# A fixed TensorE order from chunk 2 on, and two chunks' merges side by side, in a recurrence with a feed-forward block

## The chip, the core and the metric

The kernel runs on one core of a Trainium2 chip. The core has five engines with a queue each: TensorE (PE in the profile; its weight loads are PEld), VectorE (DVE), ScalarE (ACT), GpSimd (POOL) and SyncE (SP), which here only issues DMAs; ScalarE issues some too. An engine works through its queue in order, and an instruction that waits holds up all behind it. The metric is the device time of one execution in microseconds (us). Before the change it was 904.21 us, the median of 14 runs (901.24 to 910.47).

## What is computed

Batch 4, 8 heads, 768 tokens, head dimension 40, all float32. For each head a 40 x 40 state is carried over the tokens; the outputs of all heads, 320 numbers for each of 3072 tokens, go through a feed-forward block with 2048 hidden units:

```python
for t in range(S):
    y[:, :, t] = einsum('bhd,bhde->bhe', rt, state)
    Sa = einsum('bhde,bhe->bhd', state, at)
    state = state * wt[:, :, None, :] - einsum('bhd,bhe->bhde', Sa, bt)
    state = state + einsum('bhd,bhe->bhde', vt, kt)
...
x = y.transpose(0, 2, 1, 3).reshape(B * S, H * D)
h = x @ w_in
out = (h * sigmoid(h)) @ w_out
```

## The kernel before

**Chunks and units.** The 768 tokens are cut into 12 chunks of 64 (numbered 0 to 11, `n` in the code). Each chunk has two units (`m` 0 and 1), a unit being two of the four batches. Inside a chunk the recurrence is turned into matrix products and the inverse of a 64 x 64 triangular matrix for each head; only a state, the tile GV, goes from chunk to chunk.

**Prepare** (`prepare`, `pre`) readies a chunk's inputs for each unit: `scale` (two scans, L339, and a reciprocal, L340, on VectorE), `reciprocals` and `scaled` (key and query scalings on GpSimd, L352, L367 or L363), `rest` (the other keys on GpSimd, L344, two squares on ScalarE for a check, L347 and L348, and the load of w for a later unit), and `scores`, which calls `between` (TensorE products `pm`, masked by VectorE at L290) and, for the second unit, stores them to DRAM as md. `prepare(n)` returns ten steps, five for each unit, and the lists of indices in the code pick their order. Chunks 5, 7, 9 and 11 are staged: their scaled queries wait in a tile `stage`, and `stack` copies them.

**Rows** (`invert`, `inverse`). For two chunks at once the scores come back from DRAM as mi, and VectorE inverts by substitution: each `row` is a product (L423) and a reduce (L430), and each needs the one before. Chunks 0 to 3 invert blocks of 16 (15 rows), later ones blocks of 32 (31 rows). `back` copies the result into mi, half on ScalarE (L439) and half on VectorE (L440), and sends it to DRAM as xd.

**Merge** (`merge`) puts a chunk's inverse together from its blocks. `fetch` loads XT from xd; `turned` transposes blocks on VectorE (L467). For chunks below 4, `corners` (TensorE products, a VectorE scaling into the tile qq, L488) and `complete` (TensorE products, a VectorE add at L518, four ScalarE copies at L523, a GpSimd memset) join the 16-blocks to 32-blocks. `first` and `second` (products `pq` and `po`, a pair of ScalarE copies after each, L542 and L560) join the 32-blocks to 64.

**Chain** (`chain`), six steps for each unit of a chunk: `keys` (TensorE transposes `pt`), `right` (`pr`), `solve` (`pu` and `pw`, with the inverse XT), `read` (`pl`, masked at L726), `write` (`pgy`; VectorE updates the state GV at L765 and L769 and makes the output yx at L774; ScalarE's queue sends yx to DRAM as xs) and `turn` (the state transposed into GT, by VectorE in even chunks from 2 on, L691, by TensorE in odd ones). `keyed` (`pm`, L312) makes part of the input of a chunk's `right`, and runs before it.

**Feed-forward** (`moe`). A pair of chunks is 512 token columns. When both chunks are written, `fetch` loads xs back as xt (issued by ScalarE, L800 and L802). A *first step* is six products into two banks (L817, L822) and two Silus on ScalarE (L824, tile gts); a *second step* is eight products (L829) that sum over half of the hidden units, with a copy (L838, or L843 and an add on GpSimd and the stores of out). The steps of a pair are numbered from 0: first steps 0 to 3, second 4 to 7, first 8 to 11, second 12 to 15. The pair of chunks 0 and 1 is cut by chunk, so it has 24: first steps of half width 0-3, 6-9 and 12-19, second steps 4-5, 10-11 and 20-23. All wait in one list `queue`; `take(n)` emits the next n.

**Order.** A planner at compile time puts each engine's instructions in order: by their place in the program, but what it reckons to be ready goes first when the engine would be free. `in_order` ties an instruction behind the last one of its line: feed-forward products are one line from the start; with `mark["pair"]` set, `product` ties every other TensorE product to the same line, and TensorE's order is the program's order. `behind` ties one instruction behind another on the same engine. For even chunks, once `mark["pair"]` is set, the VectorE instructions of `scale` are tied so: unit 0 behind `mark["row"]`, the last reduce of the rows, and unit 1 behind `mark["across"]`, the last transpose of an even chunk's merge. Weights arrive as 64-bit words and are converted on VectorE and ScalarE in 41 steps, `convert`, during the first 210 us.

**Stages.** Chunks 0 and 1 run one after the other, with 4 steps of the first pair's queue. Then 8 more steps are woven with prepare of chunks 2 and 3, their rows and the merge of chunk 2. A loop handles chunks 2 and 3 with TensorE's order left to the planner: chunk 2's solve is followed by chunk 3's merge; prepare of chunks 4 and 5 and the rows for both are woven in; 10 of the 12 steps left are given out, 16 new ones are added, `mark["pair"]` is set and 8 are taken (L1032). The loop at L1033 then makes four passes, for chunks 4-5, 6-7, 8-9 and 10-11. Each pass takes one step at seven places along its two chains (L1042 to L1066), one more before the second chunk's write, fetches xt and adds its own pair's 16 steps, takes two, turns the state, and takes six more beside the rows of the next two chunks. Those lines end a pass (L1071 to L1073):

```python
fetch, more = moe(n, xs)
x += [partial(fetch, 0), partial(queue.extend, more), partial(take, 2)] + turn
weave(x + [partial(take, 1)] * 6, rows[1:36])
```

In the fourth pass there are no further rows; the new steps are added and `run(queue)` (L1081) empties the list: the tail.

Of the kernel before, what the change touches and what calls it, by code (L numbers as in the profile page):

```python
# [9 lines left out]
F32 = mybir.dt.float32  # L10
# [31 lines left out]
def kernel(  # L42
# [355 lines left out]
    def inverse(md, N, queue, lo=0, hi=128):  # L398
        steps = []
        xd = dr.tile([128, 32, 32], F32, name="xd", bufs=2)  # L400

        if lo == 0:
            mark["tiles"] = [sb.tile([128, 2 * SKIP], F32, name="mi"), sb.tile([128, 32 * 32], F32, name="tmp")]
        mif, tmp = mark["tiles"]
        mi = mif[:, 0 : 32 * 32].rearrange("p (s t) -> p s t", s=32)
        I = 32 // N
        tmp = tmp[:, 0 : I * N * N].rearrange("p (i s t) -> p i s t", i=I, s=N)

        def blocks(x):
            x = x.rearrange("p (i x) -> p i x", x=SKIP)[:, :, 0 : 16 * 32] if N == 16 else x[:, 0 : 32 * 32].unsqueeze(1)  # L410
            return x.rearrange("p i (s t) -> p i s t", t=32)

        X, M = blocks(XIf), blocks(mif)
        for h in range(lo, hi, 64):
            mark["mi"] = send(queue, mi[h : h + 64], md[h : h + 64]).ins
        L = slice(lo, hi)

        pin = partial(in_order, line="vector") if hi - lo == 64 else lambda x: x

        def row(t):  # L420
            n = N - 1 - t
# [8 lines left out]
            x = nc.vector.tensor_reduce(out=X[L, :, t + 1 : N, t], in_=part, axis=AX.X, op=ALU.add)  # L430
            pin(x)
            mark["row"] = x.ins

        for t in reversed(range(N - 1)):
            steps.append(partial(row, t))

        def back():
            turned = XI.rearrange("p t s -> p s t")
            nc.scalar.copy(out=mi[L, 0:16], in_=turned[L, 0:16])  # L439
            pin(nc.vector.tensor_copy(out=mi[L, 16:32], in_=turned[L, 16:32]))  # L440
            send(queue, xd[L], mi[L])

        steps.append(back)
        return steps, xd

    def merge(n, xd, queue):
# [17 lines left out]
        def turned():  # L464
            for r in range(0, 128, 32 if small(n) else 64):
                c = r % 64
                x = nc.vector.transpose(out=X[r : r + 32, :, 32 - c : 64 - c], in_=X[r : r + 32, :, c : c + 32])  # L467
                pin(x)
                if n % 2 == 0:
                    mark["across"] = x.ins  # L470
            box["qq"] = sb.tile([128, N, 48], F32, name="qq", tag="tmp" if n > 0 else "xt")


        def corners():
# [17 lines left out]
        def complete():  # L492
            pp = box["qq"][:, :, 32:48]
            pe = bank("po")
            for h in range(N):
                for r in range(0, 128, 32):
                    product(
                        nc.tensor.matmul,
                        pe[r : r + 16, h * 16 : h * 16 + 16],
                        lhsT=pp[r : r + 32, h, :],  # L500
                        rhs=X[r : r + 32, h, r % 64 + 16 : r % 64 + 32],
                        start=True,
                        stop=True,
                        tile_position=(r, r),
                    )
                for r in range(0, 128, 64):
                    product(
                        nc.tensor.matmul,
                        pe[r : r + 32, 256 + h * 16 : 272 + h * 16],
                        lhsT=X[r : r + 32, h, 0:32],  # L510
                        rhs=pp[r : r + 32, h, :],
                        start=True,
                        stop=True,
                        tile_position=(r, r),
                    )
            pe = pe.rearrange("p (z h t) -> p z h t", z=2, h=N)
            for r in range(0, 128, 64):
                pin(nc.vector.tensor_tensor(  # L518
                    out=X[r : r + 32, :, 32:48], in0=pe[r : r + 32, 1], in1=X[r : r + 32, :, 32:48], op=ALU.add
                ))  # L520
# [443 lines left out]
    for u in units[2] + units[3]:  # L964
# [7 lines left out]
    del queue[0:4]  # L972
    fetch(1)
    ahead = [prepare(n) for n in (2, 3)]
    weave(
        queue[0:8],
        [x[i] for x in ahead for i in (0, 5, 1, 6, 2, 7, 4, 9, 3, 8)] + [partial(keyed, u) for u in units[2]] + invert(3),
        convert[21:31],
    )
    del queue[0:8]  # L980
    for n in range(2, 4):
        for u in units[n]:
            load_v(u)
            load_r(u)
        for u in units[n + 2] if n == 3 else []:
            load(u)
        if n % 2 == 0:
            xs = dr.tile([DM, 4 * NM * C], F32, name="xs", bufs=2)
        steps = [x for pair in zip(*[chain(u, xs) for u in units[n]]) for x in pair]
# [16 lines left out]
        del queue[0:now]  # L1006
    for u in units[6]:
        load(u, "bk")
    fetch, more = moe(2, xs)
    fetch(0)  # L1010
    queue += more

    def each(what, n, *x):
        for u in units[n] if n < NN else []:
            what(u, *x)
# [220 lines left out]
```

## Time and profile before

| What | Value |
|---|---|
| median of 14 runs | 904.21 us (901.24 to 910.47) |
| profiled execution | 908.37 us, span 906.6 us, granted TensorE clock 0.908 |
| TensorE busy | 783.2 us, 86% of the span, 10914 instructions |
| VectorE busy | 555.7 us, 61% |
| ScalarE busy | 296.7 us, 33% |
| GpSimd busy | 150.8 us, 17% |
| chain of work that ended last | PE 52%, DVE 34%, DMA 5%, issue 3% |
| start of chunk 4's transposes | 373.3 us |
| passes of the loop, by the transposes that begin them | 124.8, 123.4 and 123.4 us, then 73.4 to the end of the last write |
| tail | from 818.2 us, 88 us |

The profile is one execution, recorded on the chip. The 40 slices are equal parts of the span; a digit is the busy share in tenths, and PEclk the granted TensorE clock in tenths. In an answer by time, a line gives the start in us, the time in us, engine, source line, operation, out<-in, shapes and count; in brackets stands how long the engine had been idle and what released it. A float32 product counts as two matmuls, so a second step is x16, a first step x8 (L817) and x4 (L822). "ACTq" is a DMA issued by ScalarE, "issue" time in which an engine waited for nothing that the profile shows. L268 is the helper `product`: go by the tile's name.

### The profile page before, as it was taken

What the parts mean: (1) busy time and instruction counts of PE and PEld (TensorE: products, weight loads), DVE (VectorE), ACT (ScalarE), POOL (GpSimd) and SP (SyncE); (2) the same over time, 40 slices, a digit from 0 to 9 for tenths busy, and PEclk for the clock granted to TensorE, in tenths of its full rate; (3) what the DMA queues carried; (4) which work ended last, traced back from release to release, by engine and by line L of the source; (5) the groups of instructions that cost most, each with busy time, mean ns of one, the idle gap of its engine ahead of it and who ended that gap; (6) DMA issues with size and microseconds to landing.
All of it is one profiled execution on the core that took longest, in us unless ns stands there. A gap on an engine that the chain in (4) does not pass through costs nothing.

```text
span 906.6 us, 25356 instructions
## 1 busy us (share of the span) xinstructions
PE 783.2 (86%) x10914; PEld 552.3 (61%) x10914; DVE 555.7 (61%) x1084; ACT 296.7 (33%) x689; POOL 150.8 (17%) x156
## 2 busy tenths in 40 slices
PE   2045689898889769999998999999999989999996
PEld 2034677675668563775854866747758557675544
DVE  9989989995107589529598276895395951610000
ACT  2234468552331311534122514115250234231120
POOL 7402024001020500224001304102140000000001
PEclk9655769999679688999999999999999999999999
DMA  8964636644033450362732454603624222202001
GB/s 171 202 144 133 155 90 158 159 124 116 19 75 84 102 138 24 68 149 67 162 86 47 109 115 93 158 8 81 142 51 112 65 47 40 55 9 72 1 1 31
DMA packets 240150, 82.99 MB, mean 92 GB/s; under 512 B 207136, under 2 KB 231968, under 8 KB 240032
## 3 DMA queue, kind: packets, MB, share of 16 engines
q1 hardware_dynamic: 219488, 69.96, 34.5%
q10 hardware_dynamic: 20544, 11.34, 4.7%
q8 instruction: 87, 1.43, 0.6%
q14 instruction: 31, 0.25, 0.1%
HBM read 67.11 MB, written 14.16 MB: 90 GB/s over the span
## 4 chain that ended last, share of the span: by engine, by line
PE 52%; DVE 34%; DMA 5%; issue 3%; SPq 3%; ACT 2%; POOL 1%; ACTq 0%; POOLq 0%; DVEq 0%
PE po L829 14%; PE ph L817 10%; DVE tmp L423 9%; DVE XI L430 8%; PE pgy L268 4%; DVE w L340 4%; PE pl L268 4%; PE ph L822 3%; PE po L268 3%; PE pm L268 3%; PE pr L268 3%; PE pq L268 3%; SPq L221 3%; PE pu L268 2%; PE pt L268 2%
## 5 line engine op out<-in xcount | busy, mean ns | idle before, releaser
L829 PE MATMUL po<-wo_s,gts 128*128 128x320 f32 x768 | 226.4, 450 | 10.0 <-ACT gts L824 8.1
L817 PE MATMUL ph<-xt,wi_s 128*128 128x512 f32 (+1 forms) x448 | 185.1, 555 | 15.1 <-DMA xt<-xs 8.8
L829 PEld LDWEIGHTS po<-wo_s,gts 128*128 128x128 f32 x768 | 146.2, 195 | 75.7 <-issue 10.9
L817 PEld LDWEIGHTS ph<-xt,wi_s 128*128 128x128 f32 x448 | 82.6, 195 | 97.4 <-issue 69.0
L824 ACT ACTIVATE gts<-ph 128x512 f32<-128x512 f32 (+1 forms) x112 | 54.5, 532 | 194.1 <-PE ph L822 192.5
L726 DVE TENSOR_TENSOR vl<-pl,ml 128x512 f32<-128x512 f32 x48 | 30.9, 685 | 111.7 <-PE pl L268 58.7
L423 DVE TENSOR_TENSOR tmp<-XI,mi 64x2 f32<-64x2 f32 (+40 forms) x169 | 84.5, 500 | 10.2 <-DMA mi<-md 5.6
L340 DVE RECIPROCAL w<-W 128x512 f32<-128x512 f32 x24 | 80.3, 3344 | 1.0
L430 DVE TENSOR_REDUCE XI<-tmp 64x2 f32<-64x2 f32 (+40 forms) x169 | 76.8, 454 | 4.8
L845 POOL TENSOR_TENSOR ot<-gts,ot 128x320 f32<-128x320 f32 x24 | 21.1, 877 | 326.5 <-ACT gts L843 326.5
L352 POOL TENSOR_TENSOR kb<-kb,w 128x512 f32<-128x512 f32 x20 | 25.4, 1269 | 217.7 <-DVE w L340 84.0
L822 PE MATMUL ph<-xt,wl_s 64*128 64x512 f32 (+1 forms) x224 | 57.9, 588 | 0.0
L268 PE MATMUL pm<-a,kb 64*64 64x64 f32 x1280 | 42.4, 247 | 16.4 <-POOL kb L370 15.5
L268 PEld LDWEIGHTS pm<-a,kb 64*64 64x64 f32 x1280 | 39.1, 160 | 22.0 <-POOL kb L370 15.7
L268 PE MATMUL pq<-XT,sb 32*32 32x32 f32 (+1 forms) x1280 | 29.9, 202 | 25.7 <-DVE XT L467 15.1
L843 ACT COPY gts<-po 128x320 f32<-128x320 f32 x24 | 10.2, 425 | 125.8 <-PE po L829 102.4
L268 PE MATMUL pl<-r,vut 64*128 64x64 f32 x768 | 46.5, 274 | 2.3 <-ACT vl L654 2.3
L367 POOL TENSOR_TENSOR a<-a,W 64x512 f32<-64x512 f32 x32 | 38.7, 1210 | 56.1 <-DMA a<-in_aT 34.1
L268 PEld LDWEIGHTS pl<-r,vut 64*128 64x128 f32 x768 | 44.7, 189 | 4.7 <-ACT vl L654 2.4
L268 PEld LDWEIGHTS pq<-XT,sb 32*32 32x32 f32 (+1 forms) x1280 | 27.1, 124 | 32.4 <-issue 15.9
L268 PE MATMUL pt<-ident,kb 128*128 128x128 f32 x192 | 26.7, 297 | 23.2 <-DVE a L312 23.2
L312 DVE TENSOR_TENSOR a<-pm,ml 64x512 f32<-64x512 f32 x48 | 33.0, 688 | 19.8 <-PE pm L268 19.1
(108 smaller groups left out, 1036.6 us busy)
## 6 DMA issues: line engine op xcount, KB each, us to landing
kb<-in_bT SPq DMA_DIRECT2D x48, 128.0 KB
vut<-in_vT SPq DMA_DIRECT2D x48, 128.0 KB
r<-in_rT SPq DMA_DIRECT2D x24, 256.0 KB
w<-in_wT SPq DMA_DIRECT2D x45, 128.0 KB
kb<-in_kT SPq DMA_DIRECT2D x44, 128.0 KB
a<-in_aT SPq DMA_DIRECT2D x32, 128.0 KB
vl<-in_v SPq DMA_DIRECT2D x48, 80.0 KB
xs<-yx ACTq DMA_DIRECT2D x48, 80.0 KB
```

Of the source, the lines that this page charges most:

```text
L221: x = queue.dma_start(out, in_)
L268: x = what(*x, **y)
L312: x = nc.vector.tensor_tensor(out=u.a[O, j], in0=pm[O].rearrange("p (q t) -> p q t", q=Q), in1=ml[O].unsqueeze(1).to_broadcast([C, Q, C]), ...
L340: pin(nc.vector.reciprocal(R, u.W[:, :, 1 : C + 1]))
L367: nc.gpsimd.tensor_tensor(out=u.a[J, j], in0=u.a[J, j], in1=u.W[J, :, 0:C], op=ALU.mult)
L423: x = nc.vector.tensor_tensor(out=part, in0=X[L, :, t + 1 : N, t + 1 : N], in1=M[L, :, t, t + 1 : N].unsqueeze(2).to_broadcast([hi - lo, I ...
L430: x = nc.vector.tensor_reduce(out=X[L, :, t + 1 : N, t], in_=part, axis=AX.X, op=ALU.add)
L726: nc.vector.tensor_tensor(out=u.vl[:, :, j, D:], in0=pl[j].rearrange("p (q t) -> p q t", q=Q), in1=ml.unsqueeze(1).to_broadcast([128, Q, C ...
L817: in_order(nc.tensor.matmul(ph[n], lhsT=wi_s[:, k, at : at + 128], rhs=xt[:, k, :], start=k == 0, stop=False))
L822: in_order(nc.tensor.matmul(ph[n], lhsT=wl_s[R, i, :], rhs=xt[R, 2, :], start=False, stop=True))
L824: nc.scalar.activation(out=place(2 * i + n)[:, T], in_=ph[n], func=AF.Silu)
L829: in_order(nc.tensor.matmul(po[:, 0:DM], lhsT=place(f)[:, b * 128 : b * 128 + 128], rhs=wo_s[:, NF // 2 * half + f, :], start=f == 0, stop ...
```

## The change

- In `back`, where the rows cover 128 partitions and blocks of 16 (chunks 2 and 3), ScalarE's half of the copy goes away and VectorE copies all of it. In every case `mark["row"]` is now VectorE's copy in `back`, and no longer the last reduce.
- The merge of chunk 3 gets its qq in another buffer (tag "mi"), and `mark["across"]` is also set by its add in `complete`.
- The weave of eight steps ends with the fetches of the inverses (`rows[0:19]`); chunk 2's merge leaves it.
- The loop over chunks 2 and 3 is replaced by a written-out order like that of the later loop, with `mark["pair"]` set from chunk 2's keys on: four steps, keys and right, then the merges of both chunks in turns, with chunk 2's solves between chunk 3's last products. `prepare(4)` comes after that and is tied behind the rows and the add as in the later passes. Feed-forward steps are taken at eight marked places, and eight more beside the rows of chunks 4 and 5. Loads of chunks 4, 5 and 6 move with it; the strict order on SP's queue (`issued["sync"]`) begins when the rows of chunks 4 and 5 fetch their scores.
- The passes from chunk 4 on are the same text as before.

```diff
         def back():
             turned = XI.rearrange("p t s -> p s t")
-            nc.scalar.copy(out=mi[L, 0:16], in_=turned[L, 0:16])
-            pin(nc.vector.tensor_copy(out=mi[L, 16:32], in_=turned[L, 16:32]))
+            at = 0
+            if N == 32 or hi - lo == 64:
+                at = 16
+                nc.scalar.copy(out=mi[L, 0:16], in_=turned[L, 0:16])
+            x = nc.vector.tensor_copy(out=mi[L, at:32], in_=turned[L, at:32])
+            pin(x)
+            mark["row"] = x.ins
             send(queue, xd[L], mi[L])
...
-            box["qq"] = sb.tile([128, N, 48], F32, name="qq", tag="tmp" if n > 0 else "xt")
+            box["qq"] = sb.tile([128, N, 48], F32, name="qq", tag={0: "xt", 3: "mi"}.get(n, "tmp"))
...
+                pin(x)
+                if n == 3:
+                    mark["across"] = x.ins
...
     ahead = [prepare(n) for n in (2, 3)]
+    rows = invert(3)
     weave(
         queue[0:8],
-        [x[i] for x in ahead for i in (0, 5, 1, 6, 2, 7, 4, 9, 3, 8)] + [partial(keyed, u) for u in units[2]] + invert(3),
+        [x[i] for x in ahead for i in (0, 5, 1, 6, 2, 7, 4, 9, 3, 8)] + [partial(keyed, u) for u in units[2]] + rows[0:19],
         convert[21:31],
     )
     del queue[0:8]
-    for n in range(2, 4):
...
-        now = {2: 6, 3: 4}[n]
-        x = prepare(n + 2)
-        if n == 2:
-            weave(steps[0:4], queue[0:1], convert[31:])
-            scores = [partial(load, u) for u in units[n + 2]] + [x[i] for i in (0, 5, 1, 6, 2, 4, 7, 9, 3, 8)]
-        else:
-            weave(steps[0:4], queue[0:1], [x[i] for i in (0, 5, 2, 7, 1, 6, 4, 9, 3, 8)])
-            scores = [partial(stack, u) for u in units[n + 2]]
-        rows = invert(n + 2)
-        merges = rows[35:]
-        weave(
-            steps[4:6] + late.pop(n, []) + [partial(keyed, u) for u in units[n + 1]] + steps[6:],
-            queue[1:now],
-            scores + rows[0:36],
-        )
-        del queue[0:now]
...
     mark["pair"] = True
+    xs = dr.tile([DM, 4 * NM * C], F32, name="xs", bufs=2)
+    keys, right, solve, read, write, turn = start(2)
+    each(load_v, 2)
+    each(load_r, 2)
+    weave(queue[0:4] + keys + right, convert[31:])
+    del queue[0:4]
+    each(load_v, 3)
+    each(load, 4)
+    each(load, 5)
+
+    one_, two = rows[19:24], late.pop(2)
+    take(1)
+    run(one_[0:2])
+    take(1)
+    run(two[0:1] + one_[2:3] + two[1:2] + one_[3:4] + two[2:3] + one_[4:5])
+    x = prepare(4)
+    run(two[3:4] + solve[0:1] + [x[i] for i in (0, 5, 1, 6)] + two[4:5] + solve[1:2] + [x[i] for i in (2, 7, 3, 8)])
+    each(keyed, 3)
+    run(read)
+    each(load_vut, 3)
+    take(1)
+    run(write + [x[i] for i in (4, 9)])
+    each(load_vl, 3)
+    x = prepare(5)
+    run([x[i] for i in (0, 2, 5, 7)] + turn)
+    keys, right, solve, read, write, turn = start(3)
+    run(keys + [x[i] for i in (1, 6)] + right)
+    take(1)
+    run(solve[0:1])
+    take(1)
+    run(solve[1:2] + [x[i] for i in (4, 9)])
+    rows = invert(5)
+    merges = rows[35:]
+    run(rows[0:1] + [x[i] for i in (3, 8)])
     issued["sync"] = mark["mi"]
     each(load_v, 4)
-    each(load_r, 4)
-    take(8)
+    each(load, 6, "bk")
+    run(read)
+    each(stack, 5)
+    x = [partial(each, load_vut, 4), partial(take, 1)]
+    x += write + [partial(each, load_vl, 4)] + [partial(keyed, u) for u in units[4]]
+    fetch, more = moe(2, xs)
+    x += [partial(fetch, 0), partial(queue.extend, more), partial(take, 2)] + turn
+    weave(x + [partial(take, 1)] * 8, rows[1:36])
```

More of the change, by code (lines that the diff above doesn't have):

```diff
@@ L517, in complete @@
             for r in range(0, 128, 64):
-                pin(nc.vector.tensor_tensor(
+                x = nc.vector.tensor_tensor(
                     out=X[r : r + 32, :, 32:48], in0=pe[r : r + 32, 1], in1=X[r : r + 32, :, 32:48], op=ALU.add
-                ))
+                )
+                pin(x)
+                if n == 3:
+                    mark["across"] = x.ins
                 nc.gpsimd.memset(X[r + 32 : r + 64, :, 0:32], 0.0)
@@ L980 @@
     del queue[0:8]
-    for n in range(2, 4):
[L982 to L989, printed above, removed]
-        now = {2: 6, 3: 4}[n]
-        x = prepare(n + 2)
-        if n == 2:
-            weave(steps[0:4], queue[0:1], convert[31:])
-            scores = [partial(load, u) for u in units[n + 2]] + [x[i] for i in (0, 5, 1, 6, 2, 4, 7, 9, 3, 8)]
-        else:
-            weave(steps[0:4], queue[0:1], [x[i] for i in (0, 5, 2, 7, 1, 6, 4, 9, 3, 8)])
-            scores = [partial(stack, u) for u in units[n + 2]]
-        rows = invert(n + 2)
-        merges = rows[35:]
-        weave(
-            steps[4:6] + late.pop(n, []) + [partial(keyed, u) for u in units[n + 1]] + steps[6:],
-            queue[1:now],
-            scores + rows[0:36],
-        )
-        del queue[0:now]
[L1007 to L1011, printed above, removed]
     def each(what, n, *x):
```

## The prediction

> **What bounds the kernel now.** I read the 40 slices first, then busy time by stage, then TensorE, ScalarE and VectorE in order of time.
>
> ```profile
> PE   2045689898889769999998999999999989999996
> DVE  9989989995107589529598276895395951610000
> PEclk9655769999679688999999999999999999999999
> ```
>
> VectorE is full to about 205 us, TensorE from about 365 us on; between them neither is, and TensorE's clock falls. By stage (columns: PE, PEld, DVE, ACT, POOL busy, clock, DMA share, GB/s):
>
> ```profile
> 214.00:373.30 159.30, 135.67 (x2269) 100.04 (x2269) 87.37 (x162) 40.44 (x94) 22.37 (x24) 0.81 0.34 77
> 373.30:498.10 124.80, 120.53 (x1602) 81.55 (x1601) 85.09 (x153) 39.69 (x89) 22.68 (x22) 0.99 0.43 97
> ```
>
> The first row is chunks 2 and 3: clock 0.81. The second is one pass of the loop for chunks 4 and 5: TensorE idles 4.3 of 124.8 us. The end of a pass, on TensorE and then on ScalarE:
>
> ```profile
> 452.79 8.88 PE L829 MATMUL po<-wo_s,gts 128*128 128x320 f32 x32
> 461.60 1.98 PE L268 MATMUL pt<-ident,GV 64*40 64x64 f32 x64
> 464.20 3.67 PE L817 MATMUL ph<-xt,wi_s 128*128 128x512 f32 x8 [0.62 <-DMA xt<-xs]
> ...
> 482.93 4.04 PE L829 MATMUL po<-wo_s,gts 128*128 128x320 f32 x14
> 490.19 6.80 PE L829 MATMUL po<-wo_s,gts 128*128 128x320 f32 x18 [3.22 <-ACT gts L824]
> 496.93 1.20 PE L268 MATMUL pq<-XT,sb 32*32 32x32 f32 x64
> ```
>
> ```profile
> 451.44 6.52 ACTq L780 DMA_DIRECT2D xs<-yx  x4
> ...
> 459.73 0.39 ACTq L800 DMA_DIRECT2D xt<-xs  x1
> ...
> 488.57 1.07 ACT L439 COPY mi<-XI 128x512 f32<-128x512 f32 x1 [4.94 <-DVE XI L430]
> 489.55 0.59 ACT L824 ACTIVATE gts<-ph 128x512 f32<-128x512 f32 x1
> ```
>
> The recurrence's output goes to DRAM (451-458), comes back as xt (issued 459.73), and the next pair's first feed-forward step starts at 464.20. Two second steps of the pair before (452.79, 8.88 us) and the turn (1.98) stand in that gap. The line at 488.57 shows the other bound: the rows' copy stands ahead of a Silu in ScalarE's queue.
>
> **The change part by part.** I add the new order from rows of before and set it against the same stretch.
>
> *The queue of steps.* After chunk 1, 12 steps remain in both. Before takes 18 of 28 (12 plus 16) by the loop's start: 10 left, as the trace shows (two second steps at 378.30 and 385.57 come first). The change takes 4, six singles, 2 and 8 = 20: 8 left. A pass takes 8, then adds 16 and takes two at once. Before, these two are old second steps; after, they are the new pair's first two first steps, which need xt. The order on TensorE is fixed, so turn, six more steps and the next merge queue behind this wait, and ScalarE's Silus and copies behind them.
>
> Chunks 2 and 3. Step 15 of the first queue ends at 211.05; the loop's first transposes are at 373.3: 162.3 us. After, up to chunk 3's transposes: keys and right 3.9 (1.90 + 2.00), three half-width first steps 7.95 (2.65 each), two corners 2.8 (1.41), two completes 5.2, four merge products 4.6 (1.15), solve 2.9, keyed 2.0, read 3.7, write 5.4, between 1.1: 39.6. Stalls: each complete shows about 2 us of issue (0.85 + 2.06 in one, 1.50 in the other): 4. Side by side, chunk 3's products cover most hops of chunk 2's merge; two stay bare, the wait of each chunk's first product for VectorE's add (0.9) and ScalarE's four copies (1.5), of which chunk 3's corners or chunk 2's second product cover about 0.9: 2 x 1.5 = 3. No wide step stands between step 17 and the read, so I take cold prices there: 0.6 to 1.0 per merge product (1.85, 2.19 at 238 and 243), 2.2 for the solve (5.1 at 312), 0.9 keyed (1.47 per 32 against 1.0): 7. Sum 53.7: chunk 3's transposes at 264.8, chunk 2's write ended at 263.7.
>
> Then VectorE and GpSimd lead: in the loop 19.2 us go by from the write's end (407.8) through scan, reciprocal and key scaling to the last reciprocal keys (427.0). So chunk 5's scores end at 283.8, three us after TensorE could. Read 3.7, second step 4.4, write 5.4, keyed 2.0: 299.4. From here as in a pass: xt after 11, four first steps 18.8 (4.69), four second 17.6 (4.40), one merge product 1.1: 347.9.
>
> The rows of chunks 4 and 5 start 9.9 after the scores (12.1 at 557.6, less the 2.2 that key loads then hold SP's queue ahead of the score stores; the change puts those loads behind the score fetch): 293.7. They take 43.8 as at 444.8 to 488.6, and 9.6 more to the transposes: 347.0. But:
>
> ```profile
> 339.07 0.59 DVE L440 COPY mi<-XI 128x512 f32<-128x512 f32 x1
> 339.57 0.42 DVE L430 TENSOR_REDUCE XI<-tmp 128x16 f32<-128x256 f32 x1
> ...
> 363.16 1.16 DVE L430 TENSOR_REDUCE XI<-tmp 128x31 f32<-128x961 f32 x1
> 364.23 1.28 DVE L339 TENSOR_TENSOR_SCAN W<-w,one 128x260 f32<-128x260 f32 x2
> ```
>
> VectorE's half of the copy runs after 15 of 31 rows, slipped between a product and its reduce. The next scan is pinned behind mark["row"], now this copy and no longer the last reduce, so 1.28 + 3.35 = 4.6 us can slip into the rows. I take it (the copy did the same): 351.6, a gain of 21.7 us. Bounds: nothing slips in, 25.4; cold and issue doubled, 15; all of VectorE's relief below arrives, 31.
>
> *Prepare(4) moves.* Two scans and reciprocals at 167.8, 169.6, 178.6, 179.8 (9.2 us), four squares on ScalarE, GpSimd's four key scalings at 202-211 and their w loads go behind the rows of chunk 3. There VectorE idles 5.3 us before the fetched inverses and more later, so they cost nothing; without that cover, 9.2. Rows 3 can then end up to 9.2 earlier (213.3), but TensorE is at 97% (150-214) with steps that need no rows, and keys, right and step 16 (6.6 after 211.05) end at 217.7, where corners could start at 222. I have used 217.7, so 4.4 is already in the sum.
>
> *Copy on one engine.* ScalarE's 1.07 beside VectorE's 0.60 becomes one VectorE copy of about 1.2: 0.1. It frees a Silu that held TensorE 2.49 at 214.67. *Second qq buffer, loads of chunks 4 and 5:* no work added; TensorE's 42 us from 222 to 264 covers their issues on SP (kb 5.2, a 3.5, GV 5 to 6). If a GV load waits on right and holds SP ahead of the inverse fetch, up to 5 us.
>
> *Three passes.* First step at 464.2, now after 11.4 us idle. Row: after 6.45 idle at 340.59 eight such products took 5.70 instead of 3.70, so 2.0 more. Then two first 9.4, turn 2.0, two first 9.4, four second 17.6: merge at 504.6, was 496.93: +7.65. The 4.6 in the rows is hidden (their inverses would serve 501.5). The 40.4 from xt to the merge added to the other passes' xt: 588.39 + 40.4 against 620.31 is +8.5, and 711.1 (issue 706.65 + the first pass's 4.47 to landing) + 40.4 against 743.71 is +7.8. Together +23.9. Bounds: 17 (never cold), 37 (the rows' copy ahead of Silus costs 4.3 in each).
>
> The Trainium skill, "TensorE: Matmul & The Clock Gate", Part 1 says that an idle window of about 3.4 us halves the clock and about 3.4 us of work restores it; this speaks against the change. By it four starts would lose at most 4 x 1.7 = 6.8 us, against 4 x 2.0 here. The trace parts from it on the gap: 2.49 us idle at 214.67 was enough (four products 1.85, were 1.13).
>
> *Tail.* Before, two second steps (8.88 at 818.20) end as xt lands; after, TensorE waits: two steps less, the same wait, 2.0 cold, 0.1 for the earlier issue: +1.9 (0 to 3).
>
> Sum: -21.7 + 23.9 + 1.9 = +4.1. The profiled execution took 908.37 us (span 906.6 and 1.8 around it), 4.2 above the median of 904.21 and inside the runs' spread (901.24 to 910.47); the difference is carried to the median: 908.3. I take 908.
>
> **Rivals.** *VectorE's relief carries through:* 9.2 us leave a full stretch, and ScalarE's Silus stop waiting on squares (2.13 and 1.27 of TensorE waits). Against: TensorE was 97% busy there. It decides once 6.8 of the 9.2 arrive (4.1 + 2.7); all of it gives 908.3 - 9.2 = 899. *The rows' copy blocks:* 488.57 stands ahead of a Silu already, and the steps come later by 11; against: with the scan the rows end later too. A second step that begins at 487 needs the last Silu by 490.6; behind a copy that starts at 493.2 it gets it at 494.9, so 4.3, and three times that: 921. *The steps don't stall:* xt is there when the two steps come up; for it only that transfers look short; against, 459.73 waits on stores that wait on the write. Then the entry's gain (21.7) and the two steps less in the tail (8.8) stay, while the scans, no longer hidden, cost 4.6 in each of two passes (9.2): 904.2 - 21.7 - 8.8 + 9.2 = 883.
>
> **How the numbers follow.** Main case 0.52, own range 901 to 915; relief 0.20; blocked copy 0.22; no stall 0.06. Two runs are told apart at 0.3% (2.7 us). Faster: 0.05 + 0.17 + 0.06 = 0.28; same: 0.15 + 0.03 = 0.18; slower: 0.32 + 0.22 = 0.54. The range 893 to 924 leaves out no stall and the far ends of two bounds (entry 15, passes 37).
>
> **What would show it.** Right: the loop's first chunk-4 transposes at 345-356; L817 idle 9 to 11 us on xt after keyed in each pass, its first products near 5.7; passes of 131 to 134 us; L339 between L423 and L430. Wrong: passes of 125, or the entry above 362 or below 342.

## The result and the profile after

The changed kernel takes 922.03 us (median of 10 runs, 916.35 to 928.44); the kernel before took 905.25 us in the same comparisons (47 runs). The ratio is 1.0188, with a 95% interval of 1.0160 to 1.0215: slower, by close to 2%. The profiled execution took 922.61 us, 920.7 of it span (before: 908.37 and 906.6). So the span grew by 14.1 us where the prediction's sum had 4.1. (The medians lie 16.8 us apart: the profile of before fell on an execution 3.1 us above the median of the 47, that of after on one 0.6 above its own.)

In the changed kernel the lines of the old code stand eight or so further down: L817 is now L825, L829 is L837, L780 is L788, L765 is L773. By stage (columns: PE, PEld, DVE, ACT, POOL busy, clock, DMA share, GB/s):

```profile
206.80:267.30 60.50, 47.97 (x1463) 42.56 (x1461) 31.25 (x50) 20.00 (x50) 11.42 (x12) 0.74 0.39 86
267.30:352.90 85.60, 82.06 (x848) 55.66 (x845) 68.99 (x123) 23.47 (x53) 16.09 (x16) 0.96 0.39 87
352.90:487.70 134.80, 121.36 (x1604) 81.90 (x1601) 86.94 (x154) 39.76 (x90) 23.63 (x23) 0.95 0.40 89
487.70:624.50 136.80, 122.10 (x1606) 82.45 (x1601) 84.36 (x152) 40.09 (x92) 23.30 (x23) 0.94 0.39 88
624.50:756.90 132.40, 121.79 (x1605) 81.87 (x1601) 76.12 (x148) 38.03 (x84) 19.52 (x20) 0.95 0.34 77
```

The first two rows are chunks 2 and 3; they end 20.4 us earlier than before (352.9 against 373.3). The other three are the passes for chunks 4 to 9: 134.8, 136.8 and 132.4 us where before they took 124.8, 123.4 and 123.4. TensorE's busy time in a pass is hardly changed (121.4 against 120.5 in the first); its idle time went from 4.3 to 13.4 us. What it waits for is the first line of the view of TensorE's waits (total, times, longest):

```profile
PE ph L825 <- DMA xt<-xs: 43.4, 5, 11.5
```

Here is the first pass on TensorE, from the key products of the next pair to the next pair's merge:

```profile
430.90 1.15 PE L268 MATMUL pm<-a,kb 64*64 64x64 f32 x32
433.43 1.15 PE L268 MATMUL pm<-a,kb 64*64 64x64 f32 x32 [1.37 <-DVE yx L782]
446.06 6.11 PE L825 MATMUL ph<-xt,wi_s 128*128 128x512 f32 x8 [11.48 <-DMA xt<-xs]
...
453.16 3.70 PE L825 MATMUL ph<-xt,wi_s 128*128 128x512 f32 x8
...
469.14 17.49 PE L837 MATMUL po<-wo_s,gts 128*128 128x320 f32 x64
486.57 1.20 PE L268 MATMUL pq<-XT,sb 32*32 32x32 f32 x64
```

Nothing stands between the key products and xt any more: 11.48 us of idle time. The first eight products after it take 6.11 us; eight of the same products take 3.70 one step later. The four second steps run without a gap (64 products in 17.49 us). ScalarE in that place:

```profile
469.25 1.09 ACT L832 ACTIVATE gts<-ph 128x512 f32<-128x512 f32 x2 [3.54 <-PE ph L830]
474.65 1.09 ACT L442 COPY mi<-XI 128x512 f32<-128x512 f32 x1 [4.32 <-DVE XI L430]
```

The rows' copy (474.65) comes behind the last Silus, not ahead of them. And VectorE ahead of the loop, where the half copy is the line at 312.79:

```profile
312.79 0.59 DVE L443 COPY mi<-XI 128x512 f32<-128x512 f32 x1
313.29 0.42 DVE L430 TENSOR_REDUCE XI<-tmp 128x16 f32<-128x256 f32 x1
313.62 0.69 DVE L339 TENSOR_TENSOR_SCAN W<-w,one 128x260 f32<-128x260 f32 x1
314.22 0.44 DVE L423 TENSOR_TENSOR tmp<-XI,mi 128x289 f32<-128x289 f32 x1
314.58 0.69 DVE L339 TENSOR_TENSOR_SCAN W<-w,one 128x260 f32<-128x260 f32 x1
315.19 0.43 DVE L430 TENSOR_REDUCE XI<-tmp 128x17 f32<-128x289 f32 x1
315.53 3.35 DVE L340 RECIPROCAL w<-W 128x512 f32<-128x512 f32 x1
```

Two scans and a reciprocal, 4.7 us of work, lie among the rows as soon as the half copy is done; passes 1 and 2 show the same, pass 3 does not.

### The profile page after: what moved, and what is told of

Its sections match the earlier page's. It is cut to its first block, busy times and chain, and to the rows that moved or that the text cites. A ratio compares the mean times of both kernels' runs of the same rounds, so it can differ in the third digit from the quotient of the medians.

```text
span 920.7 us, 25351 instructions
## 1 busy us (share of the span) xinstructions
PE 772.7 (84%) x10914; PEld 545.9 (59%) x10914; DVE 555.6 (60%) x1084; ACT 295.7 (32%) x688; POOL 150.7 (16%) x156
## 4 chain that ended last, share of the span: by engine, by line
PE 56%; DVE 26%; DMA 10%; issue 3%; ACT 2%; SPq 1%; ACTq 1%; POOLq 0%; DVEq 0%; POOL 0%
PE po L837 15%; PE ph L825 15%; DVE tmp L423 5%; DVE XI L430 5%; PE ph L830 4%; DVE w L340 4%; PE pl L268 4%; PE pgy L268 3%; DMA xs<-yx 3%; PE pu L268 3%; PE po L268 3%; PE pm L268 2%; PE pq L268 2%; PE pr L268 2%; PE pt L268 2%
## 5 line engine op out<-in xcount | busy, mean ns | idle before, releaser
L825 PE MATMUL ph<-xt,wi_s 128*128 128x512 f32 (+1 forms) x448 | 194.2, 580 | 45.4 <-DMA xt<-xs 43.4
L837 PE MATMUL po<-wo_s,gts 128*128 128x320 f32 x768 | 214.2, 436 | 0.0
L837 PEld LDWEIGHTS po<-wo_s,gts 128*128 128x128 f32 x768 | 143.6, 190 | 62.7 <-issue 4.9
L825 PEld LDWEIGHTS ph<-xt,wi_s 128*128 128x128 f32 x448 | 87.1, 204 | 128.9 <-issue 74.7
L347 ACT ACTIVATE junk<-w 128x512 bf16<-128x512 f32 x24 | 15.1, 631 | 110.6 <-DVE w L340 90.6
L851 ACT COPY gts<-po 128x320 f32<-128x320 f32 x24 | 10.2, 424 | 96.1 <-PE po L837 80.3
```

What stands on the lines that cost most here:

```text
L825: in_order(nc.tensor.matmul(ph[n], lhsT=wi_s[:, k, at : at + 128], rhs=xt[:, k, :], start=k == 0, stop=False))
L837: in_order(nc.tensor.matmul(po[:, 0:DM], lhsT=place(f)[:, b * 128 : b * 128 + 128], rhs=wo_s[:, NF // 2 * half + f, :], start=f == 0, stop ...
```

## The experiments

The theory after the result: the loop is entered with eight steps in the queue instead of ten, so each pass comes to xt with nothing to do, and that alone costs more than the entry gains. The rival: the new order on TensorE, with the merges side by side, is worse in itself. The table has the stages of every kernel's profile; they are cut where the key transposes (pt<-ident,kb) of chunks 3, 4, 6, 8 and 10 start, and the rest runs to the end of the span. The ratio is to the kernel before.

| kernel | chunk 3 at | entry (chunk 4 at) | pass 1 | pass 2 | pass 3 | rest | span | ratio (95%) |
|---|---|---|---|---|---|---|---|---|
| before | 288.4 | 373.3 | 124.8 | 123.4 | 123.4 | 161.8 | 906.6 | 1 |
| changed | 267.3 | 352.9 | 134.8 | 136.8 | 132.4 | 163.8 | 920.7 | 1.0188 (1.0160-1.0215) |
| e1: six takes | 266.9 | 352.0 | 130.2 | 130.0 | 124.3 | 161.7 | 898.3 | 0.9962 (0.9924-0.9999) |
| e2: six takes, old pin | 263.7 | 344.3 | 125.6 | 122.8 | 122.9 | 161.9 | 877.5 | 0.9757 (0.9697-0.9817) |
| e3: old pin alone | 267.1 | 349.8 | 140.7 | 136.9 | 130.8 | 165.3 | 923.5 | 1.0141 (1.0074-1.0208) |
| e4: before, ten takes | 279.0 | 371.0 | 134.6 | 135.8 | 130.8 | 163.8 | 936.0 | 1.0445 (1.0376-1.0514) |
| e5: products in the gap | 266.7 | 350.7 | 131.1 | 135.4 | 130.4 | 163.1 | 910.7 | 1.0156 (1.0066-1.0246) |
| e6: stores from GpSimd | 268.5 | 354.8 | 131.3 | 135.9 | 132.6 | 164.8 | 919.4 | 1.0172 (1.0100-1.0244) |
| e7: early scans | 274.6 | 360.7 | 135.2 | 134.0 | 132.7 | 163.5 | 926.1 | 1.0231 (1.0158-1.0303) |
| e9: merges in series | 266.8 | 356.0 | 136.8 | 136.0 | 132.7 | 164.0 | 925.5 | 1.0197 (1.0116-1.0279) |
| e10: e2 with GpSimd's stores | 269.0 | 354.5 | 126.3 | 123.9 | 123.7 | 162.2 | 890.6 | 0.9771 (0.9746-0.9796) |
| e11: seven takes, old pin | 268.9 | 348.2 | 127.7 | 131.5 | 126.9 | 163.7 | 898.0 | 0.9971 (0.9951-0.9992) |

How far a single profile may be trusted: the changed kernel, e1, e2, e3, e5 and e11 have the same program up to chunk 3's transposes, and start them between 263.7 and 268.9. An entry is therefore read to 3 us or so. The changed kernel, e7 and e9 have the same passes: the three together took 404.0, 401.9 and 405.5 us, a single pass up to 2.8 us more in one profile than in another.

### e1: six takes beside the rows

```
-    weave(x + [partial(take, 1)] * 8, rows[1:36])
+    weave(x + [partial(take, 1)] * 6, rows[1:36])
```

> The changed kernel with six instead of eight steps of the queue taken beside the rows of chunks 4 and 5, so that the loop is entered with ten steps left instead of eight and the last two steps of each pair again lie between the key products and the first product that needs xt. Theory (the passes are long because too few steps are left to cover xt): chunk 4's transposes at 348 to 352 us (the changed kernel 352.9), TensorE waits for xt 1 us or less in each pass (the changed kernel 6.1, 5.9, 6.6), passes of about 129, 128 and 124 us (134.8, 136.8, 132.4), tail after the last write 88 to 89 us (90.3), span about 895 us, ratio to the kernel before 0.98 to 0.995. Rival (the new order and the merges side by side cost the time themselves, wherever the steps lie): the passes stay at 132 us or more and the ratio at 1.01 or above.

The ratio is 0.9962, just above the 0.98 to 0.995 expected; passes 1 and 2 are 1 and 2 us longer than written down. Of the waits for xt, 43.4 us in the changed kernel, 2.2 are left, ahead of the loop; the passes are 4.6, 6.8 and 8.1 us shorter, the rest 2.1, and the entry is where it was. So two steps less ahead of the loop take 22 us off the span, and the rival, that the new order is bad in itself, is out. What TensorE meets in the first pass is the other bound:

```profile
433.37 8.88 PE L837 MATMUL po<-wo_s,gts 128*128 128x320 f32 x32
442.18 1.98 PE L268 MATMUL pt<-ident,GV 64*40 64x64 f32 x64
444.10 3.70 PE L825 MATMUL ph<-xt,wi_s 128*128 128x512 f32 x8
...
463.38 8.88 PE L837 MATMUL po<-wo_s,gts 128*128 128x320 f32 x32
479.16 0.31 PE L268 MATMUL pq<-XT,sb 32*32 32x32 f32 x2 [6.90 <-DVE XT L472]
```

Two second steps and the turn now fill the gap, and TensorE waits 6.90 us for the inverses that come from VectorE's rows instead.

### e4: the kernel before with ten takes

```
-    take(8)
+    take(10)
```

> The kernel before with ten instead of eight steps taken ahead of the loop, and nothing else of the change: the loop is entered with eight steps left. Theory (the number of steps left is what makes the passes longer, and the rest of the change earns 20 us at the entry): entry later by two steps of 4.4 us, about 382 us; TensorE waits for xt 5 to 7 us and a cold stretch of 2 us in each pass, passes longer by 7 to 10 us each, tail longer by 1.9; span 933 to 945 us, ratio 1.03 to 1.043. Rival (the number of steps left does no harm, since the same steps are only done earlier): ratio 0.997 to 1.003.

The ratio is 1.0445, just above the 1.03 to 1.043 expected, and the span 936.0. The kernel before, with nothing else changed, shows the passes of the changed one: 134.6, 135.8 and 130.8 us, and a rest longer by 2.0. The gap too:

```profile
451.55 1.85 PE L268 MATMUL pm<-a,kb 64*64 64x64 f32 x32 [1.77 <-DVE yx L774]
464.07 6.03 PE L817 MATMUL ph<-xt,wi_s 128*128 128x512 f32 x8 [10.67 <-DMA xt<-xs]
```

The sum of passes and rest is 31.6 us over before. The entry missed what was expected: 371.0, where 382 was written down. Chunk 3's transposes already started 9.4 us earlier than in the profile of before, at a higher granted clock (see the last section); from there to the entry it took 92.0 us against 84.9, 7.1 more, near the two steps of 4.4.

### e2 and e3: the pin of the scans

```
             pin(x)
-            mark["row"] = x.ins
+            if at == 0:
+                mark["row"] = x.ins
```

e2 has this and the six takes, e3 this alone.

> The kernel with six takes, and the row's mark set only in the two inverses whose copy is VectorE's alone, so that in the passes the scans (L339, L340) are held back behind the last reduction again and do not lie between the rows' instructions. Theory: with xt covered, the rows' chain is what sets the passes, so the 3 to 5 us of scans in passes 1 and 2 come off: passes of about 124.8, 123.4 and 123.4 us as before the change, entry at 347 to 352, span 880 to 888 us, ratio 0.97 to 0.98, and 4 us or more below the kernel with six takes alone. Rival (the scans lie in VectorE's idle time even then): within 2 us of the kernel with six takes alone.

> The changed kernel with the row's mark set only in the two inverses whose copy is VectorE's alone, the eight takes left. Theory (TensorE's waits for xt and the key products set the passes, and the scans are hidden beside TensorE's steps): within 2 us of the changed kernel, ratio 1.015 to 1.02. Rival (the scans between the rows, 3 to 5 us in each of passes 1 and 2, are the unpredicted part of the passes): 6 to 9 us less, ratio 1.008 to 1.012.

e2 has a ratio of 0.9757: faster than both kernels. The span, 877.5, is below the 880 to 888 expected, by an entry at 344.3 instead of 347 to 352. Its passes are those of the kernel before:

```profile
344.30:469.90 125.60, 122.39 (x1602) 83.39 (x1601) 83.97 (x151) 40.12 (x89) 22.86 (x22) 0.97 0.43 96
469.90:592.70 122.80, 118.90 (x1601) 80.58 (x1601) 84.54 (x152) 39.70 (x89) 22.70 (x22) 1.00 0.43 98
592.70:715.60 122.90, 118.99 (x1606) 80.68 (x1601) 80.18 (x150) 38.34 (x85) 20.38 (x20) 1.00 0.36 83
```

Against e1 they are shorter by 4.6, 7.2 and 1.4 us; the scans and the reciprocal among the rows were some 4.7 us in each of passes 1 and 2. The entry is 7.7 us earlier than in e1: 3.2 of it stand ahead of chunk 3's transposes already, and the other 4.5 are again the size of the scans, which are out of the rows ahead of the loop too. In e3 the same scans are out of the rows too (the first in pass 1 runs at 470.90, behind the last reduction at 469.83), yet its three passes together take 408.4 us against 404.0 in the changed kernel: nothing is gained. Its entry is 3.1 us earlier, but xt then comes 98.4 us after the start of pass 1 (93.2 in the changed kernel), which takes that back; why it comes so late there is not settled. The ratio of 1.0141 lies between what the two theories gave for e3, and its interval holds the changed kernel's 1.0188; the passes decide it. With eight steps left, TensorE and xt set the pass and the rows have time to spare; with ten, the rows set it and every us among them counts. One flaw hid the other.

### e11: seven takes, with the old pin

```
-    weave(x + [partial(take, 1)] * 6, rows[1:36])
+    weave(x + [partial(take, 1)] * 7, rows[1:36])
```

The diff is against e2.

> The kernel with the old pin of the scans and seven takes, so that nine steps are left at the loop's entry: half of the cover that the changed kernel gave up. Theory (cover is lost step by step): TensorE idles about 4 us ahead of xt in each pass, over the 2.95 us from which the first eight products were long in the runs so far, so these take 5.2 to 6.7 us; from xt to the next merge 37 us (33.3 with ten left, 40.3 with eight in the changed kernel); each pass about 4 us longer, the tail about 1; span 888 to 892 us, ratio 0.984 to 0.992. Rival (the rows of VectorE set the passes with more than 4 us to spare, so one step does no harm): within 3 us of the kernel with ten left, ratio 0.972 to 0.980.

The ratio is 0.9971: between e2 (0.9757) and e3 (1.0141), which have ten and eight steps left and the same pin; 0.984 to 0.992 was expected. Each step of cover that is missing costs about 2% here. The first product in pass 1:

```profile
439.46 5.07 PE L826 MATMUL ph<-xt,wi_s 128*128 128x512 f32 x8 [6.63 <-DMA xt<-xs]
```

I had expected 4 us of idle time; it was 6.6, 6.5 and 5.1 us. The two steps taken right before the turn are now one old second step and one new first step, and the turn (2.0 us) stands behind that first step, so it covers nothing. From xt to the next merge went 35.3, 36.6 and 36.0 us, about 1 less than expected (of the two numbers in the expectation's brackets, 33.3 is to the transposes behind the merge, 40.3 to the merge). The three passes are 14.8 us longer than e2's (12 expected), and the entry is 3.9 later than in e2's profile.

### e5: products in the gap

```
+    def warm(n):
+        t = moe_bank("ph")
+        for _ in range(n):
+            in_order(nc.tensor.matmul(t, lhsT=ident, rhs=wi_s[:, 0, 0:512], start=True, stop=True))
...
-            x += [partial(fetch, 0), partial(queue.extend, more), partial(take, 2)] + turn
+            x += [partial(fetch, 0), partial(queue.extend, more), partial(warm, 10), partial(take, 2)] + turn
...
+            warm(8)
```

> The changed kernel with products whose result nobody uses (ten in each pass, eight ahead of the tail; 128x512, about 0.43 us each) put on TensorE between the key products of the next pair and the first product that needs xt. They are work that the reference does not ask for; they fill part of the idle time, so that TensorE comes to xt with its clock up. Theory (the first eight products after the idle time cost 2.1 to 2.9 us more only because the clock has fallen): first eight products near 3.7 us instead of 6.11, 5.88, 6.61, 5.84; span 9 us below the changed kernel's 920.7, ratio to the kernel before 1.005 to 1.012. Rival (the length of these eight comes from xt landing in pieces, or from the loads of weights, and not from the clock): they stay near 6, ratio 1.017 to 1.021.

```profile
442.62 3.67 PE L825 MATMUL ph<-xt,wi_s 128*128 128x512 f32 x8 [2.05 <-DMA xt<-xs]
575.18 6.51 PE L825 MATMUL ph<-xt,wi_s 128*128 128x512 f32 x8 [3.31 <-DMA xt<-xs]
831.31 3.67 PE L825 MATMUL ph<-xt,wi_s 128*128 128x512 f32 x8 [2.90 <-DMA xt<-xs]
```

In passes 1 and 3 and in the tail the first eight products take 3.67 us, as in the middle of a run. In pass 2 the added products ended 3.31 us ahead of xt, and the eight took 6.51. The granted clock during these eight is 1.00 in pass 1 and 0.56 in pass 2 of e5, and 0.60, 0.62 and 0.55 in the three passes of the changed kernel. It is the clock, then, and neither how xt lands nor the weights. The three that came back are worth 2.44, 2.94 and 2.17, 7.6 us; passes and rest together are 7.8 us shorter than the changed kernel's (and 5.4 and 9.5 shorter than those of e7 and e9, which have the changed kernel's passes). One by one they do not match: the passes are 3.7, 1.4 and 2.0 us shorter and the rest 0.8, so the close sum is partly chance. The span's 10.0 includes an entry 2.2 earlier, which this edit does not touch. The ratio, 1.0156, is above the range expected, with an interval that holds that range's upper part and the changed kernel's ratio as well: the profile shows the price, the times alone do not.

### e6: the output's stores from GpSimd's queue

```
-                nc.sync.dma_start(out[at : at + C, :], ot[C * be : C * be + C, :])
+                nc.gpsimd.dma_start(out[at : at + C, :], ot[C * be : C * be + C, :])
```

> The changed kernel with the stores of the output issued from GpSimd's queue instead of SP's, where each waits for GpSimd's addition anyway. Theory (two second steps that come two places earlier put their stores ahead of the score stores on SP's queue; the score stores, the rows and the updates of the state behind the rows come later, and xt with them): score store after its scores by under 2.5 us in passes 1 and 2 (the changed kernel 6), rows start 2 to 4 us earlier, xt earlier by 1.5 to 4 us in passes 1 and 2, TensorE's waits of 1.4 and 2.9 us for yx gone; passes 1 and 2 shorter by 2 to 4 us each, ratio 1.009 to 1.014. Rival (something else makes the state's update late): ratio 1.017 to 1.021.

SP's queue in pass 1 of the changed kernel, and then of e6. The scores (sb) were ready at 413.7 and at 415.5:

```profile
409.38 1.16 SPq L857 DMA_DIRECT2D out<-ot  x2
...
418.41 1.21 SPq L857 DMA_DIRECT2D out<-ot  x2
419.72 2.18 SPq L221 DMA_DIRECT2D md<-sb  x4
```

```profile
417.99 2.20 SPq L221 DMA_DIRECT2D md<-sb  x4
420.24 2.36 SPq L221 DMA_DIRECT2D mi<-md  x2
```

In the changed kernel two pairs of output stores stand ahead of the score store: the first pair waits 1.6 us for GpSimd's addition, and the two issues take 2.4 us. The score store is issued 6.0 us after the scores, in e6 2.5. In pass 2 it is 6.9 against 3.8. xt comes 90.3 and 94.2 us after the pass's start, against 93.2 and 95.4: 2.9 and 1.2 us earlier, where 1.5 to 4 each was expected. The wait for yx is gone in pass 1 and halved in pass 2 (1.46). In e5, e7 and e9, which leave the stores where they were, xt comes at 91.9, 93.7 and 95.5 in pass 1 and at 93.3, 93.3 and 94.1 in pass 2: the gain in pass 1 lies outside that spread, if only by 1.6 us, the one in pass 2 does not. Passes 1 and 2 are 3.5 and 0.9 us shorter than the changed kernel's (2 to 4 each expected). The ratio, 1.0172, lies in the rival's range and does not show the gain; in this profile the entry came 1.9 later and the rest was 1.0 longer. So the mechanism is there, and is worth some 2 to 3 us in pass 1; as a gain in time it is not shown.

### e7: the scans of chunk 4 early again

```
-            if "pair" in mark and u.n % 2 == 0:
+            if "pair" in mark and u.n % 2 == 0 and u.n > 4:
```

> The changed kernel with the scans and reciprocals of chunk 4 free to go early again, as in the kernel before, where they stand among the scores of chunks 2 and 3. Theory (VectorE's relief of 9.2 us ahead of the rows of chunk 3 carries through to the inverses): rows of chunk 3 end at about 213 us instead of 207.5, first corners at 221 to 223 instead of 217.0, chunk 4's transposes 4 to 6 us later (357 to 359), ratio 1.023 to 1.026. Rival (TensorE's own work up to 217 us hides the relief): corners and transposes within 1.5 us, ratio 1.017 to 1.021.

VectorE's copy that ends the rows of chunk 3, and TensorE's first corner product, in e7:

```profile
213.62 1.08 DVE L443 COPY mi<-XI 128x1024 f32<-128x1024 f32 x1
```

```profile
222.56 0.20 PE L268 MATMUL pq<-XT,sb 16*32 16x16 f32 x2 [4.09 <-DVE XT L472]
```

In the changed kernel the copy starts at 207.52 and the first corner product at 214.70. All of the 7.9 us at the corners is passed on: chunk 3's transposes 7.3 later, the entry 7.8. The ratio, 1.0231, is as expected; the entry lost more than the 4 to 6 I had written.

### e9: the two merges in series

```
-    run(two[0:1] + one_[2:3] + two[1:2] + one_[3:4] + two[2:3] + one_[4:5])
+    run(one_[2:5] + two[0:5])
...
-    run(two[3:4] + solve[0:1] + [x[i] for i in (0, 5, 1, 6)] + two[4:5] + solve[1:2] + [x[i] for i in (2, 7, 3, 8)])
+    run(solve[0:1] + [x[i] for i in (0, 5, 1, 6)] + solve[1:2] + [x[i] for i in (2, 7, 3, 8)])
```

> The changed kernel with the merges of chunks 2 and 3 one after the other on TensorE, chunk 2's first, and nothing else of the order moved. Theory (side by side, the products of the one cover the hops through VectorE and ScalarE of the other: four hops of 1 to 2.5 us in each merge, half of them covered): chunk 3's transposes 4 to 8 us later (271 to 275 instead of 267.3) and all that follows with them, ratio 1.023 to 1.028. Rival (the hops are short, or the entry hangs on the rows of chunks 4 and 5): within 1.5 us, ratio 1.017 to 1.021.

Chunk 3's transposes start at 266.8 against 267.3, and the bulk of the corner products (122 in a row) at 215.87 against 216.99: from there to there 50.9 against 50.3 us. The nine profiles with the merges side by side, the changed kernel's among them, have 49.9 to 51.2 us for that stretch. So putting the merges side by side gains nothing that can be seen, and not 4 to 8 us; the rival has it. TensorE's idle time in the stretch is 10.1 us in series and 8.8 to 9.9 in the nine, so hardly any hop was covered; the granted clock is 0.77 in series and 0.70 to 0.73 in the nine. Why the hops stay bare is not shown. The entry 3.1 us later comes from elsewhere, the read of chunk 3 and the second step that follows (first e9, then the changed kernel):

```profile
284.07 6.20 PE L268 MATMUL pl<-r,vut 64*128 64x64 f32 x62 [0.64 <-DVE sb L290]
290.20 7.08 PE L837 MATMUL po<-wo_s,gts 128*128 128x320 f32 x16
```

```profile
284.62 3.79 PE L268 MATMUL pl<-r,vut 64*128 64x64 f32 x64
288.34 4.57 PE L837 MATMUL po<-wo_s,gts 128*128 128x320 f32 x16
```

The same products, 13.3 us against 8.4, at a granted clock of 0.58 against 1.00 from 287 to 297. e10 shows the same slow stretch, so it isn't the order of the merges.

### e10: the fastest kernel with GpSimd's stores

The diff is e2's and e6's together.

> The kernel with six takes and the old pin of the scans, and besides it the stores of the output issued from GpSimd's queue instead of SP's. Theory (with ten steps left the stores of the second steps already stand behind the score stores on SP's queue, and only one of 0.6 us lies between the two score fetches): 0 to 1 us less in each pass, span 874 to 878 us, ratio 0.970 to 0.978, no difference from the kernel with SP's stores that can be told. Rival (the stores on SP still hold up the rows, the chain that now sets the passes): 4 us or more less, ratio under 0.971.

The ratio is 0.9771 (0.9746 to 0.9796), e2's is 0.9757: no difference. The passes (126.3, 123.9, 123.7) are not shorter than e2's either. With ten steps left the output's stores already stand behind the score stores. The span, 890.6, is outside what was expected: chunk 3's transposes at 269.0 (e2: 263.7) and the slow stretch named above (5.96 and 7.34 us for the same two groups) put the entry 10.2 us later. With its narrower interval, e10 is the better evidence that ten steps and the old pin make the kernel 2% faster than before; it holds the moved stores as well, which make no difference that can be told.

## Why the prediction was right in direction and short in size

*The entry* was right: 20.4 us earlier, 21.7 predicted, transposes at 352.9 inside 345 to 356. The way there was right as well: chunk 3's transposes at 267.3 (264.8), the rows of chunks 4 and 5 from 297.2 (293.7), the scan and reciprocal that slip into the rows. Inside it two errors cancelled. VectorE's relief, of which "4.4 is already in the sum", is worth 7.9 at the corners by e7: without it they start at 222.6 (222 predicted), with it at 214.7 and not at 217.7, since TensorE had done its own work earlier too: keys, right and step 16 ended at 213.3. The prediction had held against this that TensorE was at 97% from 150 to 214; 0.97 is the granted clock of that stretch, and TensorE was busy for 58.1 of the 64 us, 91%. In e7, with the scans early again, chunk 2's transposes start at 211.95 instead of 206.81. From the corners to chunk 3's transposes the merges, the solve and the write took 52.6 us, where 47.1 was worked out: the side-by-side order, which was to cover most hops, gains nothing by e9, and the clock in that stage is 0.74.

*The tail* was right: from the last write's end to the end 90.3 against 88.4, +1.9 as predicted.

*The three passes* are the term that failed: +32.4 instead of +23.9. What the step did from xt on was right. xt to the next merge took 40.5, 40.3 and 41.0 us, 40.4 predicted, clock included: the first eight cost 2.4, 2.2 and 2.9 us more than 3.7, where 2.0 was taken from one row of before. What was wrong is the other half of the same step: it added the 40.4 to the times at which xt had come in the kernel before. Counted from the pass's start it had xt at 90.9, 90.3 and 89.7 us; after the change xt came at 93.2, 95.4 and 90.2. These 7.8 us are nearly the whole difference of 8.5. Of them 1.8 are a misreading: 588.39 is where TensorE began to wait in pass 2 of the kernel before, and not where xt came:

```profile
590.16 3.67 PE L817 MATMUL ph<-xt,wi_s 128*128 128x512 f32 x8 [1.76 <-DMA xt<-xs]
```

So xt came at 92.1 there, and the step should have given +25.7. The other 6 us are real: xt came 2.3, 3.3 and 0.5 later than before (2.7 to 7.3 in all in the profiles of e5, e7 and e9, so the size is known roughly). e6 names the cause for pass 1, where it puts xt back to 90.3: the second steps of the pair before, two places earlier in the queue, put their output stores ahead of the score stores on SP's queue; the rows start later against the chain (427.21, the chain's write at 425.59; in before the rows came first, 444.81 and 445.47), VectorE works on the first rows when the state's update comes up, and yx, xs and xt follow late. I had looked for what stands behind TensorE's wait on TensorE and ScalarE, and had followed SP's queue at the entry only, not in the loop. The later xt of pass 2 is not settled beyond the 1.2 us of e6. e4, which has the same short queue in the old order, has xt at 93.1, 93.5 and 89.6 and nearly as long passes (401.2 us for the three, 404.0 in the changed kernel), so most of the delay belongs to the queue and not to the new order. (The bound "never cold" should read 18 and not 17, 23.9 less three times 2.0.)

*The rivals.* That VectorE's relief carries through beyond the 4.4 came true by 3.0 us at the corners, short of the 6.8 from which it was to decide, and the slower merges used that up. By the prediction's own numbers it could not have decided: its 899 takes off all 9.2 us from a sum that has 4.4 of them already, and only 4.8 were left. That the rows' copy blocks ScalarE's Silus is refuted by the trace of after: the copy (474.65) comes behind the Silus and the four second steps have no gap; its 921 is near the measured time for another reason. That the steps don't stall is refuted by 11.48, 10.66 and 9.71 us of idle time.

The main case's own range, 901 to 915, missed the 922.0; the whole range, 893 to 924, held it close to its upper end. That end owes its height to the rival of the blocked copy (921), and the copy did not block: that the range held is in part luck. Of the signs named ahead, the entry, the idle times (11.5, 10.7 and 9.7 us) and the scans among the rows came as written or close to it; the passes of 131 to 134 us did in one of three. Of the 14.1 us in the span, 4.1 were predicted, 8.5 are the passes, 1.3 the entry; the tail added nothing, and rounding the rest.

## What to carry over

When work is taken earlier to fill a wait at the entry of a loop, count what is left in the queue at the first point inside the loop where it was the cover: here two steps of 4.4 us decided, with the old pin, between 2.4% faster and 1.4% slower (e2 and e3), and the kernel before, with only that count changed, became 4.5% slower. When a step changes its place, follow its stores on their in-order queue in every pass, not only at the place of the edit. A second flaw can be free as long as the first one sets the pass (the scans among the rows: nothing at eight steps, 5 and 7 us in two passes at ten), so after undoing one, measure the other again. And when an arrival is read from an engine's wait, take the end of the idle time and not its start.

## What was not expected of the hardware

The first eight products of a feed-forward step after idle time took 3.67 us or 5.1 to 6.8, and nothing between. In the profiles of this case, 34 of 34 after 2.95 us of idle time or more were long, and 11 of 12 after 1.1 to 2.90 us were short (the exception: 5.37 after 2.03 in e10). Steps of half width are not counted here; one of them was long after 2.49 us (the kernel before, at 214.67). Among the long ones the length has nothing to do with how long TensorE was idle: 6.51 after 3.31 us, 5.16 after 11.10, 6.78 after 11.76. The Trainium skill, "TensorE: Matmul & The Clock Gate", Part 1, puts the window at about 3.4 us and calls it free-running, so that the same kernel shows a different number of slow products from run to run. The spread agrees with that, and the step lies a little below its figure here. The loss at a start, 1.4 to 3.1 us in the 34 and 2.4, 2.2, 2.9 and 2.2 in the changed kernel, is mostly over the 1.7 that the prediction had worked out from this page as the most.

The granted clock of stretches full of small products differs from profile to profile with the same instructions. From chunk 2's key transposes to chunk 3's, the kernel before took 43.6 us (244.8 to 288.4) at a clock of 0.76; e4, with the same program up to there, took 37.7 us at 0.88. In e9 and e10 a wait of 0.64 us for the scores was followed by some 10 us at a granted clock of about 0.6, 4.9 us lost; in the changed kernel there was neither the wait nor the slow stretch. A profile of one execution can be off by 5 to 10 us here, as much as several of the effects above.
